# Pairing blocks of FFN channels: gate and value products over two PSUM banks, elementwise instructions over 1024 columns

## Chip, cores, metric

One core of one Trainium2 chip. Times are device microseconds (us) of that core, from the first to the last instruction of one execution. Times are medians of several executions; the profile is of one of them.

## The reference

```python
def mab(q, kv):                                  # attention, 4 batches of 12416 rows of 128
    s = (q @ kv.transpose(0, 2, 1)) / sqrt(C)
    a = softmax(s)
    return a @ kv
h = mab(I, x)                                    # 32 inducing rows attend to x
y = mab(x, h).reshape(B * N, C)                  # x attends to the 32 rows of h

xn = y / sqrt(mean(y * y) + 1e-6) * rms_g        # then a SwiGLU FFN over 49664 rows
g, val = xn @ w_gate, xn @ w_val                 # 128 -> 1536, twice
out = (silu(g) * val) @ w_out                    # 1536 -> 128
```

Almost all the work is the FFN: three products of 49664 x 128 x 1536, in fp32.

## The kernel before

Rows are handled in 100 units of up to 512 rows (25 a batch, 4 batches). The 1536 channels of a unit are 12 blocks of 128, so there are 1200 slots. In each slot TensorE does one gate product, one value product and, for a block that was finished some slots ago, one output product. ScalarE computes the SiLU, VectorE multiplies.

```python
ps_gv = pool("ps_gv", 4, space=PSUM)             # four tiles, of one bank each, in turn
...
for j in range(NJ):                              # 12 blocks of one unit
    g = ps_gv.tile([P, 512], F32, name="gv", tag="gv")
    nc.tensor.matmul(g[:, 0:T], sg[:, ts(j, P)], a[:, 0:T], start=True, stop=True)
    sl = silp.tile([P, 512], F32, name="silu")
    nc.scalar.activation(sl[:, 0:T], g[:, 0:T], AF.Silu)
    products(j)                                  # 0, 1 or 2 output products that are due
    v = ps_gv.tile([P, 512], F32, name="gv", tag="gv")
    nc.tensor.matmul(v[:, 0:T], sv[:, ts(j, P)], a[:, 0:T], start=True, stop=True)
    t = up.tile([P, 512], F32, name="u")
    nc.vector.tensor_tensor(out=t[:, 0:T], in0=sl[:, 0:T], in1=v[:, 0:T], op=ALU.mult)
    steps(j)                                     # attention of the next batch, seams, stores
```

PSUM is the memory into which TensorE puts its products; each of the four tiles above is one bank of it, 512 columns.

An output product is either plain (fp32) or split: the operand is converted into three parts of the type fp32r, and three matmuls of 0.23 us take the place of one of 0.85 us (the prediction reads both from the trace). The conversion takes two ScalarE copies and two GpSimd subtractions a block:

```python
def three(j, t):
    n = kws["n"] = (kws.get("n", 0) + 1) % 4
    hi, lo, d = (kws[name][:, n, 0:T] for name in ("hi", "lo", "d"))
    v = t[:, 0:T]
    nc.scalar.activation(hi, v, AF.Copy, scale=1.0 - 2.0 ** -13)
    nc.gpsimd.tensor_tensor(out=lo, in0=v, in1=hi.bitcast(F32), op=ALU.subtract)
    def rest():                                  # one slot later
        hs = third.tile([P, 512], F32, name="hs")
        nc.scalar.activation(hs[:, 0:T], hi.bitcast(F32), AF.Copy, scale=1.0 + 2.0 ** -12)
        nc.gpsimd.tensor_tensor(out=d, in0=hs[:, 0:T], in1=v, op=ALU.subtract)
        kara.append((ready[b, u, j], lambda: project3(j, hi, lo, d)))
```

A plan made ahead of time decides which blocks are converted: `SLOT` is the assumed length of a slot, `SPLIT` the GpSimd time of one conversion, `RESERVE` the number of due products above which a slot takes two. The plan converts 383 of the 1200 blocks and leaves 36 slots without an output product.

## Time and profile before

| | before |
|---|---|
| time, median | 1709.84 us (1709.16 to 1710.18, 3 runs) |
| first gate product | 59.8 us |
| loop, first to last gate product | 1640.7 us |
| of it TensorE's own work (matmuls at their pitches) | 1557.1 us |
| of it waits (the rest) | 83.6 us |
| after the last gate product | 7.6 us |

The loop's two parts are my arithmetic on the trace: the number of matmuls of each form times the start-to-start distance of that form where nothing waits, and what remains. The same prices are used for every kernel; what a lowered clock adds to matmuls counts as waits. TensorE's work is most of the time, so a kernel with the same work can win 84 us at most in the loop.

In the view of waits a line reads: engine, tile and line that waited, what ended the wait, then us in all, number of waits, and the longest.

### The profile page before, as it was taken

To read this page: it belongs to the slowest core of one execution; us is meant where nothing else is said; L and a number is where in the kernel's file an instruction comes from. 1 tells how busy PE (TensorE), PEld (TensorE's weight loads), DVE (VectorE), ACT (ScalarE), POOL (GpSimd) and SP (SyncE) were. 2 spreads that over 40 slices of the span, in tenths; PEclk is the share of its full clock that TensorE was granted. 3 is DMA by queue.
4 is the path that set the end of the run, shared out by engine and by line. 5 is a ranking of instruction groups with operands and counts; after the bars stand their busy time and mean duration, and the time that the engine had idled before them with its cause. 6 is when DMAs were issued, how large, how long until landed. Compare 5 with 4: busy or idle time off the path is not lost.

```text
span 1708.1 us, 23142 instructions
## 1 busy us (share of the span) xinstructions
PE 1668.0 (98%) x6781; PEld 1036.0 (61%) x6781; DVE 1145.0 (67%) x1914; ACT 1224.3 (72%) x2179; POOL 1146.2 (67%) x919
## 2 busy tenths in 40 slices
PE   8799999999999999999999999999999999999998
PEld 7445565655566666665556666566556666666666
DVE  4767775676667776667666777566756666666665
ACT  4446777676787777766678777767677887788786
POOL 1217775677587777677658777577657878887774
PEclk9899999999999999999999999999999999999999
DMA  6344533533354332433335314153211111111111
GB/s 261 74 68 75 70 80 60 121 75 69 56 78 68 49 65 51 105 75 88 65 57 90 57 34 87 28 131 79 54 31 33 35 36 33 33 36 36 33 37 24
DMA packets 389358, 112.64 MB, mean 66 GB/s; under 512 B 365136, under 2 KB 369776, under 8 KB 386672
## 3 DMA queue, kind: packets, MB, share of 16 engines
q1 hardware_dynamic: 388944, 111.02, 33.1%
q8 instruction: 54, 0.88, 0.2%
q14 instruction: 72, 0.59, 0.1%
q10 hardware_dynamic: 288, 0.15, 0.0%
HBM read 53.95 MB, written 27.00 MB: 47 GB/s over the span
## 4 chain that ended last, share of the span: by engine, by line
PE 87%; ACT 4%; DVE 3%; issue 2%; POOL 2%; DMA 1%; SPq 1%; ACTq 0%; DVEq 0%; POOLq 0%
PE acc L560 40%; PE gv L610 16%; PE gv L615 14%; PE u L578 5%; PE u L576 5%; PE mm L310 2%; DVE u L617 1%; PE mm L485 1%; ACT silu L612 1%; PE mm L368 1%; DVE aT L507 1%; PE gv L301 1%; ACT hi L510 1%; ACT hs L602 1%; POOL xn L603 1%
## 5 line engine op out<-in xcount | busy, mean ns | idle before, releaser
L617 DVE TENSOR_TENSOR u<-silu,gv 128x512 f32<-128x512 f32 (+2 forms) x1200 | 790.7, 666 | 512.1 <-PE gv L615 262.6
L612 ACT ACTIVATE silu<-gv 128x512 f32<-128x512 f32 (+2 forms) x1200 | 696.6, 584 | 370.1 <-PE gv L610 326.2
L560 PE MATMUL acc<-u,wo 128*128 128x512 f32 (+2 forms) x1634 | 811.5, 581 | 4.4 <-DVE u L617 3.1
L615 PE MATMUL gv<-a,sv 128*128 128x512 f32 (+2 forms) x1200 | 774.1, 645 | 3.7 <-DVE u L617 3.5
L598 POOL TENSOR_TENSOR xn<-u,xn 128x512 fp32r<-128x512 f32 (+2 forms) x383 | 482.2, 1259 | 356.0 <-ACT xn L597 295.1
L610 PE MATMUL gv<-a,sg 128*128 128x512 f32 (+2 forms) x1200 | 490.2, 409 | 12.8 <-ACT silu L612 8.5
L603 POOL TENSOR_TENSOR xn<-hs,u 128x512 fp32r<-128x512 f32 (+2 forms) x383 | 481.9, 1258 | 23.2 <-ACT hs L602 22.0
L610 PEld LDWEIGHTS gv<-a,sg 128*128 128x128 f32 x1200 | 227.2, 189 | 259.3 <-ACT silu L612 127.5
L560 PEld LDWEIGHTS acc<-u,wo 128*128 128x128 f32 x1634 | 305.1, 189 | 84.6 <-issue 18.2
L615 PEld LDWEIGHTS gv<-a,sv 128*128 128x128 f32 x1200 | 227.2, 189 | 204.1 <-issue 141.9
L597 ACT ACTIVATE xn<-u 128x512 fp32r<-128x512 f32 (+2 forms) x383 | 237.0, 619 | 15.6 <-DVE u L617 13.9
L602 ACT ACTIVATE hs<-xn 128x512 f32<-128x512 f32 (+2 forms) x383 | 235.7, 615 | 4.5 <-POOL xn L603 3.1
L560 PE MATMUL acc<-xn,xn 128*128 128x512 f32 (+2 forms) x383 | 149.7, 391 | 6.1 <-POOL xn L603 6.1
L578 PE MATMUL u<-xn,xn 128*128 128x512 f32 (+2 forms) x383 | 149.2, 390 | 0.0
L576 PE MATMUL u<-xn,xn 128*128 128x512 f32 (+2 forms) x383 | 147.8, 386 | 0.0
L499 POOL TENSOR_TENSOR rs<-ms,mhalf 128x16 f32<-128x16 f32 (+2 forms) x28 | 75.5, 2696 | 35.3 <-DVE ms L497 34.9
L560 PEld LDWEIGHTS acc<-xn,xn 128*128 128x128 f32 x383 | 71.8, 187 | 25.7 <-POOL xn L603 10.5
L578 PEld LDWEIGHTS u<-xn,xn 128*128 128x128 f32 x383 | 71.9, 188 | 15.6
L576 PEld LDWEIGHTS u<-xn,xn 128*128 128x128 f32 x383 | 72.1, 188 | 14.0
L569 DVE STREAM_TRANSPOSE o<-o 128x512 f32<-128x512 f32 (+2 forms) x97 | 67.7, 698 | 3.4
L568 DVE TENSOR_TENSOR o<-acc,o 128x512 f32<-128x512 f32 (+2 forms) x97 | 64.9, 669 | 0.0
L581 ACT ACTIVATE o<-u 128x512 f32<-128x512 f32 (+2 forms) x97 | 56.4, 581 | 0.2
(153 smaller groups left out, 735.0 us busy)
## 6 DMA issues: line engine op xcount, KB each, us to landing
out_dram<-o SPq DMA_DIRECT2D x320, 64.0 KB, 2.0
xT<-in_x_dram SPq DMA_DIRECT2D x60, 256.0 KB, 4.9
xn<-in_x_dram SPq DMA_DIRECT2D x60, 256.0 KB, 4.7
a<-hi SPq DMA_DIRECT2D x160, 64.0 KB, 2.0
a<-lo SPq DMA_DIRECT2D x158, 64.0 KB, 2.0
w<-w SPq DMA_DIRECT2D x22, 256.0 KB, 3.2
xn<-in_x_dram SPq DMA_DIRECT2D x5, 1024.0 KB, 10.9
out_dram<-o SPq DMA_DIRECT2D x64, 60.0 KB, 2.0
```

The source lines that it names most:

```text
L499: nc.gpsimd.tensor_tensor(out=rs, in0=ms, in1=mhalf[rows, 0:n], op=ALU.pow)
L560: nc.tensor.matmul(acc[:, 0:T], lhsT, rhs, start=st["left"] == NJ, stop=st["left"] == 1)
L576: nc.tensor.matmul(ups[:, 0:T], w[:, i, :], hi, start=st["k"] == nk, stop=False)
L578: nc.tensor.matmul(ups[:, 0:T], w[:, NK + i, :], lo, start=False, stop=not st["k"])
L597: nc.scalar.activation(hi, v, AF.Copy, scale=1.0 - 2.0 ** -13)
L598: nc.gpsimd.tensor_tensor(out=lo, in0=v, in1=hi.bitcast(F32), op=ALU.subtract)
L602: nc.scalar.activation(hs[:, 0:T], hi.bitcast(F32), AF.Copy, scale=1.0 + 2.0 ** -12)
L603: nc.gpsimd.tensor_tensor(out=d, in0=hs[:, 0:T], in1=v, op=ALU.subtract)
L610: nc.tensor.matmul(g[:, 0:T], sg[:, ts(j, P)], a[:, 0:T], start=True, stop=True)
L612: nc.scalar.activation(sl[:, 0:T], g[:, 0:T], AF.Silu)
L615: nc.tensor.matmul(v[:, 0:T], sv[:, ts(j, P)], a[:, 0:T], start=True, stop=True)
L617: nc.vector.tensor_tensor(out=t[:, 0:T], in0=sl[:, 0:T], in1=v[:, 0:T], op=ALU.mult)
```

## The change

The intent: ScalarE, VectorE and GpSimd pay a fixed part for every instruction (0.15 to 0.18 us, as the prediction works out from the trace), so handle two blocks with one instruction of 1024 columns. Gate products of a pair fill banks 0 and 1, value products banks 2 and 3. With the time saved on GpSimd the plan converts more blocks (470). Cut to its core:

```diff
-    SLOT, SPLIT, RESERVE = 1.25, 2.75, 3
+    SLOT, UPPER, SPLIT, RESERVE = 1.25, 2.6, 4.85, 3
-    ps_gv = pool("ps_gv", 4, space=PSUM)
+    ps_gv = pool("ps_gv", 1, space=PSUM)
+    gv = ps_gv.tile([P, 4, 512], F32, name="gv")
+    us = up.tile([P, 8, 512], F32, name="u")
     # one tile of the prologue:
-            return ps_gv.tile([P, 512], F32, name="gv", tag="gv")
+            kws["bank"] = (kws.get("bank", -1) + 1) % 4
+            return gv[:, kws["bank"], :]
     # the loop:
-        for j in range(NJ):
-            g = ps_gv.tile([P, 512], F32, name="gv", tag="gv")
-            nc.tensor.matmul(g[:, 0:T], sg[:, ts(j, P)], a[:, 0:T], start=True, stop=True)
-            ... SiLU, products(j), value product, multiplication, steps(j): one block
+        for j in range(0, NJ, 2):
+            pair = range(2)
+            for i in pair:
+                nc.tensor.matmul(gv[:, i, 0:T], sg[:, ts(j + i, P)], a[:, 0:T], start=True, stop=True)
+            sl = silp.tile([P, 2, 512], F32, name="silu")
+            nc.scalar.activation(sl[:, :, 0:T], gv[:, 0:2, 0:T], AF.Silu)
+            products(j)
+            for i in pair:
+                nc.tensor.matmul(gv[:, 2 + i, 0:T], sv[:, ts(j + i, P)], a[:, 0:T], start=True, stop=True)
+            slot = uslots.pop(0)
+            uslots.append(slot)
+            nc.vector.tensor_tensor(out=slot[0][:, :, 0:T], in0=sl[:, :, 0:T], in1=gv[:, 2:4, 0:T], op=ALU.mult)
+            steps(j)
+            products(j + 1)
+            steps(j + 1)
     # the conversion: hi, lo, hs and d over both blocks of a pair, rest() two slots later
     # cut: x rows of batches 1 to 3 loaded in halves into one buffer; z multiplied on VectorE
```

## The prediction

> **What bounds the kernel now.** I read the page's head first (busy shares), then its chain of waits, then ten microseconds of the timeline in the steady state, then the groups by form. The page first:
>
> ```profile
> PE 1668.0 (98%) x6781; PEld 1036.0 (61%) x6781; DVE 1145.0 (67%) x1914; ACT 1224.3 (72%) x2179; POOL 1146.2 (67%) x919
> PE 87%; ACT 4%; DVE 3%; issue 2%; POOL 2%; DMA 1%; SPq 1%; ACTq 0%; DVEq 0%; POOLq 0%
> ```
>
> TensorE is on 87% of the chain that ends last; no other engine has over 4%. The 98% is not proof, because matmul ends are modelled, so I take the period of a slot (one block of 128 FFN channels) from start to start in the timeline:
>
> ```profile
> 1003.20 0.39 PE L610 MATMUL gv<-a,sg 128*128 128x512 f32 x1
> 1003.43 1.02 PE L560 MATMUL acc<-u,wo 128*128 128x512 f32 x2
> 1003.88 0.79 PE L615 MATMUL gv<-a,sv 128*128 128x512 f32 x1
> 1004.51 0.40 PE L610 MATMUL gv<-a,sg 128*128 128x512 f32 x1
> 1004.75 0.39 PE L576 MATMUL u<-xn,xn 128*128 128x512 f32 x1
> 1004.98 0.40 PE L578 MATMUL u<-xn,xn 128*128 128x512 f32 x1
> 1005.21 0.39 PE L560 MATMUL acc<-xn,xn 128*128 128x512 f32 x1
> 1005.44 0.39 PE L615 MATMUL gv<-a,sv 128*128 128x512 f32 x1
> 1005.67 0.40 PE L610 MATMUL gv<-a,sg 128*128 128x512 f32 x1
> ```
>
> A slot whose output product is plain fp32 takes 1004.51 - 1003.20 = 1.31 us; one whose product is split into three fp32r matmuls takes 1005.67 - 1004.51 = 1.16 us, five matmuls 0.23 us apart. So a plain product costs 1.31 - 0.46 = 0.85 us, a split one 0.70 us, and a conversion gains 0.15 to 0.16 us. There is no gap in either slot: TensorE runs end to end.
>
> How much waiting is left? The loop runs from the first gate matmul at 59.8 us to the last at 1700.5: 1641 us. Its matmuls at those pitches (0.23 us for 512 columns, 0.217 for 480, 0.118 for 256): gate and value about 538; 817 plain products (642, 142 and 33 of the three widths) 546 + 114 + 14 = 674; 383 split ones (318, 50, 15) 221 + 33 + 5 = 259; the attention of the next batch, by the excess of the slots that hold it, about 88 (an estimate). Sum 1559, so some 82 us are waits, about 27 of them before 140 us, where the weights are still being prepared, and some 6 a batch around the two long exponentials.
>
> **What the Trainium skill says.** "TensorE: Matmul & The Clock Gate", section "Back-to-back issue gap", has N/2.4 + 2.5 ns, 216 ns at 512 columns. The plain product agrees if it is four passes (0.85/4 = 0.21 us); the fp32r matmuls here are at 0.23, and I use that. "VectorE: DVE Perf Modes", section on the TRN2 errata, has (N+151)/0.96 ns for an fp32 two-tensor operation: 691 at 512 (trace 682), 1224 at 1024. "ScalarE: Activation LUTs", "What ACT_TABLE_LOAD costs", has 186 + 0.833 N ns with immediate scale and bias: 613 at 512 (trace 597 to 631), 1039 at 1024. "GPSIMD Engine Reference", section 3.1, has about 2.6 cycles of 1.2 GHz an element for two inputs, 2.17 ns. The trace agrees, as the two widths of each group show:
>
> ```profile
> L617 DVE TENSOR_TENSOR u<-silu,gv 128x512 f32<-128x512 f32 x960 | 648.4, 682 | 409.0 <-PE gv L615 208.7 <-ACT hs L602 71.1 <-ACT xn L597 66.0
> L612 ACT ACTIVATE silu<-gv 128x512 f32<-128x512 f32 x960 | 570.6, 597 | 309.7 <-PE gv L610 269.2 <-DVE u L617 9.0 <-DVE xn L539 1.9
> L598 POOL TENSOR_TENSOR xn<-u,xn 128x512 fp32r<-128x512 f32 x318 | 410.2, 1290 | 272.5 <-ACT xn L597 219.8 <-PE gv L610 50.0 <-PE u L576 0.2
> L617 DVE TENSOR_TENSOR u<-silu,gv 128x256 f32<-128x256 f32 x48 | 19.4, 416 | 14.4 <-PE gv L610 5.5 <-PE gv L615 3.4 <-ACT silu L612 3.2
> L612 ACT ACTIVATE silu<-gv 128x256 f32<-128x256 f32 x48 | 18.2, 379 | 9.2 <-PE gv L610 9.0
> L598 POOL TENSOR_TENSOR xn<-u,xn 128x256 fp32r<-128x256 f32 x15 | 11.0, 733 | 10.2 <-ACT xn L597 10.1
> ```
>
> The number after each busy time is the mean of one instruction in ns. From 256 to 512 columns they grow by 266, 218 and 557 ns, so the fixed parts are only 150, 161 and 176 ns, and 1024 columns should take 1.21 us on VectorE, 1.03 on ScalarE and 2.40 on GpSimd.
>
> **The change, part by part.**
> *Elementwise work.* 1200 SiLU become 600: 1200 fixed parts of 0.16 become 600, ScalarE saves about 96 us; VectorE saves 600 x 0.15 = 90. Both are off the path, so this alone is worth next to nothing.
> *More split products.* The order in which the changed program's instructions compile has 470 split products (394, 64 and 12 of the three widths) where there were 383, and 730 plain ones for 817. TensorE saves 76 x 0.16 + 14 x 0.15 - 3 x 0.08 = 14.0 us. This is the one term that lies straight on the path. It is small: the pairing lets 87 more products convert, and each gives only a sixth of a slot. It isn't free: GpSimd does 235 pairs x 2 x about 2.35 = 1105 us for 964, ScalarE's two copies 490 for 473. GpSimd would then be busy about 1255 us (its multiplication of z, some 32 us, moves to VectorE), 74% of the span. It stays below TensorE.
> *Half the slack in PSUM.* Before, four single banks rotate, so a gate product waits for the SiLU of two slots earlier. Now gate and value have one pair of banks each. The next gate pair waits for this pair's SiLU: from the end of the second gate matmul 0.26 us until ScalarE starts (the timeline shows about that for an idle engine), 1.03 of work, 0.05 to pass on: 1.34 us. What TensorE has in between is the value pair (0.46) and the products placed around it. With two products that is 1.86 to 2.17 us: no wait. With none it waits 0.88 us. Likewise a value pair waits for the last multiplication, 0.26 + 1.21 + 0.05 = 1.52 us, against 0.46 plus the products. Counting in the compiled order the pairs without attention matmuls that fall short: 20 by a missing gate cover, 40 by a thin value cover of one product, together 29 us (some 9 us in each of the first three batches less the start, 2 in the last). The kernel before also has about 35 slots without a product, and pays about 0.4 us each, some 14 us, part of the 82.
> *Queues.* An operation of another kind in front of a multiplication now delays 1024 columns. In the compiled order about 30 stretches between two multiplications hold three VectorE instructions (2.1 us), some 25 hold four or five. With 1.21 for the multiplication, three make 3.3 against a pair's 2.3 to 2.6 plus a slack of 0.3 to 0.65: about 0.3 us lost each, 9 us; four or five lose 0.5 to 1.2 us (the squares' matmul there lengthens the pair), 17 us. The same clusters stand behind perhaps 25 of the 82 us now, in slots that run 0.2 to 0.5 us long.
> *The rest.* x rows of later batches are loaded in halves into one buffer five slots ahead, 6 us, for DMAs that land in 4.7 us now at twice the size, and their order lets them start earlier: no wait expected. The ramp before 59.8 us is unchanged; the last pair's drain is about 1 us longer.
> *Sum.* 1709.8 - 14 (split products) + 15 (thin pairs beyond what empty slots cost now) + 1 (clusters beyond now) + 1 (drain) = 1713. A reason to go lower: the schedule's constants look fitted to the new durations (4.85 us for two GpSimd instructions, which I get as 4.80), and the prologue and part of the thin pairs may be hidden by stalls that happen anyway, since two waits in the same place do not add. I take off half of the thin pairs' 15 us: 1705.
>
> **The rivals.**
> *A: overheads vanish and waiting shrinks.* With 186 us of fixed costs gone from ScalarE and VectorE, queues could be shorter, and the 55 us of waits after the ramp could fall by 20 to 30: 1665 to 1680. For it: waits on VectorE and ScalarE make up 7% of the chain. Against it: the longer single instruction and the halved bank rotation make each wait longer.
> *B: the rotation becomes the bound.* If SiLU or the multiplication regularly came late, each of 600 pairs would lose perhaps 0.1 to 0.2 us: 1750 to 1810. For it: only 0.3 us of slack where both products are split, and in the densest stretches ScalarE has 1.03 + 1.06 + 0.59 us a pair of about 2.4. Against it: the average pair is 2.6 us long.
> *C: GpSimd becomes the bound where conversions are dense.* 4.80 us for each two pairs of 4.9 to 5.2; a late difference blocks ScalarE's second copy, whose buffer is now single, and through it SiLU. The planner skips conversions when GpSimd is late, so I expect 5 to 10 us at the most from this: 1715.
>
> **Range and chances.** The sure term is -14, the unsure ones -10 to +25 in sum: 1688 to 1726 as 8 in 10, 1705 the middle. 2% faster would be under 1676, which needs rival A nearly in full; 2% slower, over 1744, needs rival B. Faster 0.05, within 2% 0.90, slower 0.05.
>
> **What would show it right or wrong.** Right: L652 near 1.21 us, L644 near 1.03, the two GpSimd lines near 2.40; a pair of gate starts about 2.62 us apart with two plain products, 2.31 with two split ones; new waits of TensorE's gate on SiLU and of its value pair on L652, of 20 to 50 us in all; TensorE still above 85% of the chain. Wrong: waits of gate or value matmuls above 60 us (rival B), split products waiting for GpSimd or ScalarE waiting for it by more than 15 us (rival C), or pair periods at the ideal nearly everywhere with waits well below today's (rival A). If instructions across two banks took longer than the slope says, the whole sum would be off upward.

## More of the kernel before

Before the change the gate product's weight load (PEld) waits for the SiLU that last read its bank, a short time:

```profile
PEld gv L610 <- ACT silu L612: 127.5, 458, 1.6
```

458 waits of 0.28 us on average. A weight load often waits while the matmul before it still runs, so most of this costs nothing: the gate matmuls themselves stood idle for that SiLU for 8.5 us in all.

## The result

The changed kernel takes 2565.16 us (2563.54 to 2567.95, 4 runs) against 1709.5 us for the kernel before in the same rounds: a ratio of 1.5007 (95% interval 1.4981 to 1.5033). Here and below the ratio is the mean time of one kernel's fast runs over that of the other's of the same rounds, so not quite the ratio of the medians quoted. The prediction said 1705. All outputs are right.

Busy times and the chain of waits of the changed kernel, in the order of the two lines that the prediction shows of before:

```profile
PE 2003.3 (78%) x6868; PEld 1019.7 (40%) x6868; DVE 1124.8 (44%) x1360; ACT 1181.8 (46%) x1282; POOL 1259.1 (49%) x596
PE 44%; DVE 26%; ACT 22%; issue 6%; DVEq 1%; POOL 0%; DMA 0%; ACTq 0%; POOLq 0%
```

No engine is busy for much more than three quarters of the span, and the chain that ends last is shared by three engines. That is the sign of work that goes round in a ring: not one engine is too slow, each waits for another. The groups say that the single instructions are as long as predicted (1.00 us for the SiLU and 1.19 for the multiplication, means over all widths; the 1024-column forms have 1.024 and 1.221):

```profile
L644 ACT ACTIVATE silu<-gv 128x1024 f32<-128x1024 f32 (+1 forms) x600 | 599.1, 999 | 1063.9 <-PE gv L642 1024.9
L652 DVE TENSOR_TENSOR u<-silu,gv 128x1024 f32<-128x1024 f32 (+2 forms) x482 | 574.5, 1192 | 1078.3 <-PE gv L647 1068.9
```

The waits name the ring:

```profile
PEld gv L647 <- ACT silu L644: 595.5, 592, 4.3
PEld gv L642 <- DVE u L652: 518.6, 461, 3.3
```

L642 is the gate pair, L644 its SiLU, L647 the value pair, L652 the multiplication. Both lines are wrong for a kernel with separate banks. The value product has no need of the SiLU: it writes other banks than the SiLU reads. The gate product of the next pair has no need of the multiplication. Yet 592 of 600 value pairs wait for the SiLU, and 461 gate pairs for the multiplication (115 more stand under another tile name of the product). In the timeline (start, length, engine, line; in brackets the idle time before and what ended it) one pair looks like this:

```profile
1504.08 0.74 PE L642 MATMUL gv<-a,sg 128*128 128x512 f32 x2 [0.52 <-DVE u L652]
...
1504.85 1.03 ACT L644 ACTIVATE silu<-gv 128x1024 f32<-128x1024 f32 x1 [2.00 <-PE gv L642]
...
1505.93 0.30 PEld L647 LDWEIGHTS gv<-a,sv 128*128 128x128 f32 x2 [0.16 <-ACT silu L644]
1506.04 0.62 PE L647 MATMUL gv<-a,sv 128*128 128x512 f32 x2
...
1506.80 1.22 DVE L652 TENSOR_TENSOR u<-silu,gv 128x1024 f32<-128x1024 f32 x1 [2.78 <-PE gv L647]
1508.08 0.30 PEld L642 LDWEIGHTS gv<-a,sg 128*128 128x128 f32 x2 [1.38 <-DVE u L652]
```

Gate pair at 1504.08, SiLU to 1505.88, value pair from 1505.93, multiplication 1506.80 to 1508.02, next gate pair at 1508.08: four steps in a row, 4.00 us, with no overlap among them. It does not matter what products TensorE does in between: 117 pairs with two plain products have a median period of 3.96 us, 90 pairs with two split ones 3.99. Predicted were 2.62 and 2.31. 600 pairs of 4 us make 2400 us.

| | before | changed | difference |
|---|---|---|---|
| first gate product | 59.8 | 101.7 | +42 |
| TensorE's own work in the loop | 1557.1 | 1541.6 | -15 |
| waits in the loop | 83.6 | 912.5 | +829 |
| after the last gate product | 7.6 | 8.9 | +1 |

The first line is, for the most part, the same cause in the prologue, whose transposes take their PSUM banks from the same tile (30 of the 42 us go with it in split_gv below). In the view by windows (columns: window, length, then busy us and number of instructions of PE, PEld, DVE, ACT and POOL, then the granted clock, DMA share and GB/s) the kernel before and the changed one have, from 10 to 60 us:

```profile
10.00:60.00 50.00, 45.52 (x497) 35.45 (x498) 31.70 (x70) 22.88 (x45) 8.02 (x5) 0.97 0.52 189
```

```profile
10.00:60.00 50.00, 32.15 (x123) 15.25 (x123) 8.75 (x22) 12.20 (x21) 2.54 (x2) 0.52 0.39 145
```

A quarter of the matmuls in the same time, and TensorE's clock granted at 0.52 instead of 0.97.

### The profile page after: what moved, and what is told of

Same layout as the page of the kernel before. It is cut to its first block, busy times and chain, and to the rows that moved or that the text cites. A ratio compares the mean times of both kernels' runs of the same rounds, so it can differ in the third digit from the quotient of the medians.

```text
span 2564.7 us, 21399 instructions
## 1 busy us (share of the span) xinstructions
PE 2003.3 (78%) x6868; PEld 1019.7 (40%) x6868; DVE 1124.8 (44%) x1360; ACT 1181.8 (46%) x1282; POOL 1259.1 (49%) x596
## 4 chain that ended last, share of the span: by engine, by line
PE 44%; DVE 26%; ACT 22%; issue 6%; DVEq 1%; POOL 0%; DMA 0%; ACTq 0%; POOLq 0%
ACT silu L644 20%; DVE u L652 17%; PE gv L647 16%; PE gv L642 15%; PE acc L579 6%; DVE xn L652 4%; PE mm L327 1%; PE u L595 1%; PE u L597 1%; PE mm L500 1%; PE gv L318 1%; DVE o L587 1%; DVE aT L523 1%; DVE o L588 1%; DVEq L652 1%
## 5 line engine op out<-in xcount | busy, mean ns | idle before, releaser
L644 ACT ACTIVATE silu<-gv 128x1024 f32<-128x1024 f32 (+1 forms) x600 | 599.1, 999 | 1063.9 <-PE gv L642 1024.9
L652 DVE TENSOR_TENSOR u<-silu,gv 128x1024 f32<-128x1024 f32 (+2 forms) x482 | 574.5, 1192 | 1078.3 <-PE gv L647 1068.9
L621 POOL TENSOR_TENSOR xn<-u,xn 128x1024 fp32r<-128x1024 f32 (+1 forms) x191 | 441.7, 2313 | 611.7 <-ACT xn L620 370.6
L642 PE MATMUL gv<-a,sg 128*128 128x512 f32 (+2 forms) x1200 | 455.2, 462 | 303.2 <-DVE u L652 237.8
L647 PE MATMUL gv<-a,sv 128*128 128x512 f32 (+2 forms) x1200 | 459.0, 465 | 222.7 <-ACT silu L644 222.7
L579 PE MATMUL acc<-u,wo 128*128 128x512 f32 (+2 forms) x1164 | 599.2, 600 | 1.0 <-POOL wo L279 1.0
L629 POOL TENSOR_TENSOR xn<-xn,u 128x1024 fp32r<-128x1024 f32 (+1 forms) x191 | 444.0, 2325 | 182.4 <-ACT xn L628 182.2
L642 PEld LDWEIGHTS gv<-a,sg 128*128 128x128 f32 x1200 | 190.6, 196 | 660.1 <-DVE u L652 518.6
L647 PEld LDWEIGHTS gv<-a,sv 128*128 128x128 f32 x1200 | 191.0, 195 | 605.8 <-ACT silu L644 595.5
L652 DVE TENSOR_TENSOR xn<-silu,gv 128x1024 f32<-128x1024 f32 (+2 forms) x118 | 138.7, 1176 | 258.5 <-PE gv L647 246.1
L628 ACT ACTIVATE xn<-xn 128x1024 f32<-128x1024 f32 (+2 forms) x235 | 242.6, 1032 | 0.0
L620 ACT ACTIVATE xn<-u 128x1024 fp32r<-128x1024 f32 (+1 forms) x191 | 197.1, 1032 | 62.3 <-PE u L595 62.3
L579 PE MATMUL acc<-xn,wo 128*128 128x512 f32 (+2 forms) x296 | 149.8, 589 | 0.4 <-DVE xn L652 0.4
```

The lines of the kernel that those rows point to most:

```text
L579: nc.tensor.matmul(acc[:, 0:T], lhsT, rhs, start=st["left"] == NJ, stop=st["left"] == 1)
L620: nc.scalar.activation(hi[:, :, 0:T], v, AF.Copy, scale=1.0 - 2.0 ** -13)
L621: nc.gpsimd.tensor_tensor(out=lo[:, :, 0:T], in0=v, in1=hi[:, :, 0:T].bitcast(F32), op=ALU.subtract)
L628: nc.scalar.activation(hs, hi[:, :, 0:T].bitcast(F32), AF.Copy, scale=1.0 + 2.0 ** -12)
L629: nc.gpsimd.tensor_tensor(out=d[:, :, 0:T], in0=hs, in1=v, op=ALU.subtract)
L642: nc.tensor.matmul(gv[:, i, 0:T], sg[:, ts(j + i, P)], a[:, 0:T], start=True, stop=True)
```

## The experiments

**Theory T** was that the four banks are one tile to the layer that records the program, and that it makes the waits for a tile as a whole: a write to bank 2 waits for the last reader of any bank of `gv`. The compiled program agrees: all 600 value pairs carry a wait for the SiLU of their own pair, and 595 of the 600 gate pairs one for the multiplication of the pair before. **The rivals**: the banks are waited for one by one and a pair of banks is simply too little (my prediction's rival B, R2 in the text below), an instruction that reads two banks keeps TensorE from writing the others (R1), or another part of the change costs the time (conversions, halved loads, z on VectorE). All the kernels below ran on chips next to the kernel before, whose median there was 1708.6 to 1709.5 us.

| run | median us | ratio to before (95%) |
|---|---|---|
| split_gv | 1798.57 | 1.0525 (1.0510 to 1.0541) |
| before_one_tile | 3452.64 (one run) | - |
| split_gv_alt | 1790.63 | 1.0477 (1.0461 to 1.0492) |
| unpaired_psum | 1749.35 | 1.0233 (1.0216 to 1.0250) |
| unpaired_r4 | 1745.07 | 1.0208 (1.0191 to 1.0225) |
| unpaired_s131_r3 | 1810.51 | 1.0590 (1.0571 to 1.0608) |
| unpaired_s131_r4 | 1801.75 | 1.0535 (1.0516 to 1.0555) |
| unpaired_halfcopies | 1752.08 | 1.0255 (1.0239 to 1.0271) |
| unpaired_halfall | 1740.38 | 1.0185 (1.0171 to 1.0199) |
| unpaired_sparse65 | 1733.25 | 1.0144 (1.0130 to 1.0157) |
| unpaired_stagger | 1747.85 | 1.0228 (1.0211 to 1.0245) |
| stagger_388 | 1722.71 | 1.0077 (1.0061 to 1.0093) |
| stagger_388_r3 | 1738.07 | 1.0171 (1.0156 to 1.0186) |
| stagger_dve | 1758.49 | 1.0289 (1.0275 to 1.0303) |
| unpaired_seam30 | 1738.42 | 1.0169 (1.0152 to 1.0186) |
| before_z | 1702.88 | 0.9967 (0.9955 to 0.9980) |
| before_zd | 1704.07 | 0.9973 (0.9959 to 0.9987) |

### split_gv: two tiles instead of one

```diff
-    gv = ps_gv.tile([P, 4, 512], F32, name="gv")
+    gvs = [ps_gv.tile([P, 2, 512], F32, name=n) for n in ("gvg", "gvv")]
-            return gv[:, kws["bank"], :]
+            return gvs[kws["bank"] // 2][:, kws["bank"] % 2, :]
     # gate, SiLU: gvs[0]; value, multiplication: gvs[1]
```

> The changed kernel, with its four PSUM banks as two tiles of two banks (gate, value) in place of one tile of four; same instructions, same order. Theory T: in the changed kernel the value pair waits for this pair's SiLU and the next gate pair for this pair's multiplication, because waits are made for a whole PSUM tile; banks that nobody else touches are waited for. Then this run falls to what my prediction added up, 1688 to 1726 us, the granted clock goes back to 0.99, and gate matmuls wait for SiLU alone and value matmuls for the multiplication alone, 20 to 50 us in all. Rival R1, an elementwise read across two PSUM banks keeps TensorE from writing the others: stays near 2560. Rival R2, one pair of banks each is too little to rotate with, whatever the tiles: over 1750.

Measured: 1798.57 us. Nothing but the tile that the banks belong to was changed (TensorE's instructions stand in the same order in both traces), and 767 of the 856 us are gone. The waits now have the right names, the value pair waiting for the multiplication and the gate pair for the SiLU:

```profile
PEld gvv L647 <- DVE u L652: 116.1, 268, 3.4
PEld gvg L642 <- ACT silu L644: 69.0, 71, 4.3
```

In the compiled program no value pair waits for a SiLU any more, and 599 of the 600 gate pairs wait for the SiLU of the pair before. First gate product at 72.1 us, waits in the loop 171.7 us. So T is shown, for the most part of the loss (741 us of it in the loop, 30 in the prologue, by the profiled executions), and R1, which stays near 2560, fell. But T's figure of 1688 to 1726 us was missed, and the time is over R2's mark of 1750. What is left is 89 us.

### before_one_tile: the same fault in the kernel before

```diff
-    ps_gv = pool("ps_gv", 4, space=PSUM)
+    ps_gv = pool("ps_gv", 1, space=PSUM)
+    gv4 = ps_gv.tile([P, 4, 512], F32, name="gv")
-            g = ps_gv.tile([P, 512], F32, name="gv", tag="gv")     # and v, and the prologue's
+            g = gv_bank()                                          # gv4[:, turn % 4, :]
```

> The kernel before, with its four single-bank PSUM tiles for gate and value as one tile of four banks used in the same rotation; no pairs, no wide instructions. T: a slot becomes a chain, gate 0.23 + 0.26 to start ScalarE + SiLU 0.60 + 0.05, value 0.23 + 0.26 + multiplication 0.68 + 0.05, 2.36 us a slot; times 1164 slots of 512 columns, and 68 us around the loop, about 2810 us. R1 and R2 need the 1024-column instructions or fewer banks: 1710 us.

Measured: 3452.64 us, one run. No pairs here, no longer conversions: the tile alone doubles the time of the kernel before. (A pair does the ring once for two blocks, so the single blocks suffer more.) The waits:

```profile
PEld gv L617 <- DVE u L624: 1453.2, 1191, 2.8
PEld gv L622 <- ACT silu L619: 664.2, 1106, 4.2
PE gv L617 <- DVE u L624: 862.2, 1105, 2.4
```

Of 1200 gate products 1191 wait for the multiplication, as T says. The size was not what I had worked out, 2810 us. The granted clock accounts for about half of that. In the slices of the span, in tenths of full speed:

```profile
PEclk6878988997589997998758998999776898998855
```

The mean was 0.828 (0.995 in the kernel before). I had put in matmuls at full speed. A slot of 512 columns with one plain product takes 2.47 us where the trace has the clock at full speed (median of 439), near my 2.36, and 3.71 us where it is halved (34 such slots). By such a comparison of all slots the lowered clock costs some 300 of the 640 us that I was short (an estimate from these slots); the rest is slots longer than 2.36 us at full clock, and the prologue (first gate product at 102.1 us).

### split_gv_alt and unpaired_psum: the halved rotation

split_gv_alt is split_gv with the prologue's banks taken from the two tiles in turn:

```diff
-            return gvs[kws["bank"] // 2][:, kws["bank"] % 2, :]
+            return gvs[kws["bank"] % 2][:, kws["bank"] // 2, :]
```

> split_gv, but the ramp before the loop takes its PSUM banks alternately from the two tiles, where split_gv takes both banks of one tile in a row. If waits are made for a whole PSUM tile also between the banks of a two-bank tile, split_gv's ramp is serialised by halves (its first gate matmul starts at 72.1 us, 58.1 in unpaired_psum), and this run starts its loop near 60 us and takes 1785 to 1790 us. If the ramp's delay has another cause: 1798 again.

Measured: 1790.63 us, 8 less; the first gate product is at 65.3 us instead of 72.1. unpaired_psum gives gate and value back their four single banks in turn, one block an instruction for SiLU and multiplication; conversions stay in pairs of 1024 columns:

```diff
+            for i in pair:
+                g = ps_gv.tile([P, 512], F32, name="gv", tag="gv")
+                ... gate product, SiLU into sl[:, i, 0:T]
+                products(j + i)
+                v = ps_gv.tile([P, 512], F32, name="gv", tag="gv")
+                ... value product, multiplication into slot[0][:, i, 0:T]
+                steps(j + i)
```

> The changed kernel's conversions in pairs (470 split products, 1024-column copies and differences on SBUF), but gate, value, SiLU and multiplication one block at a time over four rotating single-bank tiles, as before. Nothing waits for a bank it does not use, and the rotation is as deep as before. T with my sum: -14 us of TensorE work against the kernel before and no loss by thin pairs, 1690 to 1705 us; it should be 5 to 20 us below split_gv, which is what the halved rotation costs. If the conversions in pairs bring waits of their own (GpSimd 2.4 us an instruction), 1705 to 1730 us. R1: also near 1700, so this run does not speak on it.

Measured: 1749.35 us, 41 below split_gv_alt, though it does 600 more instructions on each of two engines. It was to be 1690 to 1705, or 1705 to 1730 with waits for the conversions: both missed. First gate product 58.1 us against 65.3, waits 139.5 us against 171.1. So even with proper waits the pairing costs 41 us: 7 in the prologue, which has four single banks in turn again, 31 in the loop and 2 after it in the profiled executions. That TensorE has less to do, with two banks a side, while it waits for the longer instruction is the likely reason in the loop. It is not shown apart: this run shortens the instructions, deepens the rotation and puts the output products at other places, all at once.

What is left is 40 us over the kernel before, with 14 us less of TensorE work: 56 us more of waits. This is the residual, and all the rest is about it. Its first candidate: the paired plan leaves 98 slots without an output product, 36 before.

### unpaired_r4, unpaired_s131_r3, unpaired_s131_r4: slots without a product

```diff
-    SLOT, UPPER, SPLIT, RESERVE = 1.25, 2.6, 4.85, 3      # unpaired_psum: 470 conversions, 98 empty slots
+    SLOT, UPPER, SPLIT, RESERVE = 1.25, 2.6, 4.85, 4      # unpaired_r4: 470, 65
+    SLOT, UPPER, SPLIT, RESERVE = 1.31, 2.6, 4.85, 3      # unpaired_s131_r3: 482, 226
+    SLOT, UPPER, SPLIT, RESERVE = 1.31, 2.6, 4.85, 4      # unpaired_s131_r4: 482, 73
```

> unpaired_psum with the stock of products that is kept back raised from 3 to 4. The same 470 split products, but in the compiled order 65 slots without an output product in place of 98 (the kernel before has 36). Theory E: a slot without a product costs 0.57 us (62 such slots of the loop lose 35.6 us in unpaired_psum), since gate and value alone don't cover the way through SiLU and the multiplication: 33 x 0.57 = 19 us less, about 1730 us. Rival: the 40 us over the kernel before are waits for GpSimd's long instructions or for the halved row loads, and stay: 1745 to 1752.

> unpaired_psum planned with slots of 1.31 us: 482 split products in place of 470 (2 us less of TensorE work), but 226 slots without a product, each next to one with two. Theory E: 128 more such slots at 0.4 to 0.57 us, 50 to 73 us more, about 1800 to 1820 us. Rival (uneven products cost nothing): 1747.

> The same 482 split products as unpaired_s131_r3, stock kept back 4: 73 slots without a product. Theory E: close to unpaired_r4, 1730 to 1740 us, 70 to 85 us below unpaired_s131_r3 with equal work on every engine. Rival: equal to it.

Measured: 1745.07, 1810.51 and 1801.75 us. unpaired_s131_r3 landed where theory E put it, but by luck: the theory, that each empty slot costs about half a microsecond, fell with the other two. 33 empty slots fewer are worth 4 us (the runs of unpaired_r4 spread over 7), 153 fewer 9 us. The waits moved to slots that do have a product. But the denser plan of 482 conversions, with 73 empty slots, is 52 us slower than unpaired_psum with 98 (its plan also assumes longer slots). So look at the conversions.

### unpaired_halfcopies, unpaired_halfall: is it the length of one instruction?

```diff
-            nc.scalar.activation(hi[:, :, 0:T], v, AF.Copy, scale=1.0 - 2.0 ** -13)
+            for i in range(2):
+                nc.scalar.activation(hi[:, i, 0:T], v[:, i, :], AF.Copy, scale=1.0 - 2.0 ** -13)
     # hs likewise; in unpaired_halfall also lo and d on GpSimd
```

> Unpaired gate and value (1749.35 us, 1.0233 of the kernel before), but each of the two ScalarE conversion copies of a pair is written as two instructions of 512 columns (about 0.6 us each) instead of one of 1024 (1.05 us). GpSimd keeps its 1024 columns. Theory G1, a SiLU stands behind a long copy in ScalarE's queue and the gate product two slots on waits for it: the 62 us of TensorE waits that go to the SiLU fall to about 40 and the time to about 1730 (1.012). Theory G2, what is late is the GpSimd result and not the SiLU: within 5 us of 1749. Theory R, the rest of the loss is the halved row loads and the plan's order, not the length of an instruction: within 5 us of 1749 too. TensorE's own work is the same, 1543 us in the loop, in all.

> The same, and the two GpSimd instructions of a pair are two of 512 columns each as well (about 1.27 us instead of 2.37). The first half of a pair's low part and difference is ready 1.1 us earlier. G1: as the last, 1730, for GpSimd adds under 3 us. G2: the waits that go to GpSimd, 11.5 us of the loop, and some of those under the products fall, so that this is 10 us or more below the last. R: within 5 us of 1749.

Measured: 1752.08 and 1740.38 us. Halving ScalarE's copies in place does nothing (G1's figure was 1730). Halving GpSimd's wins 9 us over unpaired_psum and 12 over unpaired_halfcopies, as G2 said.

### unpaired_sparse65: fewer conversions

```diff
-    SLOT, UPPER, SPLIT, RESERVE = 1.25, 2.6, 4.85, 3      # 470 conversions, 98 empty slots
+    SLOT, UPPER, SPLIT, RESERVE = 1.25, 2.6, 6.5, 3       # 268 conversions, 56 empty slots
```

> Unpaired gate and value with the spacing between two conversions in the plan raised from 4.85 to 6.5 us: 268 split products instead of 470. TensorE's own work grows by about 202 x 0.22 = 44 us, to about 1587 us in the loop. G (both): the waits beyond it, 139.5 us now, fall in step with the 202 conversions fewer, by about 55 us x 202/470 x 2 or so = 45 us, so the time stays near 1749 (1735 to 1760). R: the waits stay near 139 us, so the time is about 1793 (1.049).

Measured: 1733.25 us. TensorE has 33 us more to do (1575.6 us; I had put 44), and the kernel is 16 us faster all the same: waits 88.5 us instead of 139.5. Rival R, at 1793, fell. In these plans conversions beyond some number cost more in waits than the 0.16 us that each saves TensorE; the empty slots fell too, from 98 to 56.

### unpaired_stagger and stagger_388: bunching or number?

The halved copies of the last pair of runs still stand side by side ahead of the same SiLU, so that test of bunching was poor. unpaired_stagger puts them one slot apart, with TensorE's order the same instruction by instruction:

```diff
+            head(0)                                # hi, lo of the first block
+            soon(1, lambda: head(1))               # of the second, one slot later
+            soon(2, lambda: rest(0))               # hs, d
+            soon(3, lambda: rest(1))
-    SLOT, UPPER, SPLIT, RESERVE = 1.25, 2.6, 4.85, 3      # unpaired_stagger: 470 conversions, 98 empty slots
+    SLOT, UPPER, SPLIT, RESERVE = 1.25, 2.6, 5.4, 4       # stagger_388: 388, 67
```

> Unpaired gate and value, the same 470 conversions, TensorE's order unchanged instruction for instruction; but each conversion instruction covers one block of 512 columns and the two blocks of a pair are one slot apart, so that one copy (0.6 us) stands between two SiLUs where two (1.2 us, or one of 1.05) stood. Theory B, bunching: it is the elementwise work of two blocks standing together in ScalarE's order that makes a SiLU late; the 61 us of waits that go to the SiLU fall to 30 to 40 and the time from 1740 (all halved in place) to 1712 to 1722. Theory D, density: it is the 470 conversions as such; within 5 us of 1740.

> The same with the spacing of two conversions raised to 5.4 us and the reserve to 4: 388 split products, nearly the 383 of the kernel before, and 67 slots without a product (36 before). TensorE's own work is then 1556 us in the loop against 1557 before. B and D: waits of 85 to 100 us, as before has 84, so 1708 to 1724 us (1.0 to 1.009). Theory R, the halved row loads or another part of the change that all these kernels share: the waits stay near 125 to 130 us and the time near 1747.

Measured: 1747.85 and 1722.71 us. B, bunching, fell: one copy between two SiLUs is no better than two together (1740.38 in unpaired_halfall; D's figure, within 5 us of that, was missed by 3). R's figure for stagger_388, 1747, fell as well. With about the number of conversions of the kernel before the residual is down from 40 to 13 us: waits 97.0 us, TensorE's own work 1556.0. Since both the number and the empty slots changed, one more run was needed.

### stagger_388_r3: number or empty slots?

```diff
-    SLOT, UPPER, SPLIT, RESERVE = 1.25, 2.6, 5.4, 4       # stagger_388: 388 conversions, 67 empty slots
+    SLOT, UPPER, SPLIT, RESERVE = 1.25, 2.6, 5.4, 3       # 388 conversions, 125 empty slots
```

> stagger_388 (1722.71 us, 67 slots without a product, reserve 4) with the reserve back at 3: the same 388 conversions, but 125 slots without a product. If the number of conversions is what counts: within 6 us of 1723. If it is the empty slots (58 more, up to 0.5 us each): 1738 to 1750, as unpaired_stagger with its 470 conversions and 98 empty slots had 1748.

Measured: 1738.07 us. Of the 25 us between unpaired_stagger and stagger_388, 10 come with the smaller number (at 27 more empty slots), 15 with 58 fewer empty slots, 0.26 us a slot. So both count. Together with unpaired_r4 (33 slots, 4 us) it means that an empty slot has no fixed price: it costs where something else is late there.

### stagger_dve: is GpSimd full?

In the last quarter of the run, where no attention of a next batch is in the way, GpSimd is the busiest engine after TensorE. The last line of the view by windows, eight windows of 30 us from 1420 to 1660, for the kernel before, unpaired_psum, unpaired_stagger and stagger_388:

```profile
sum 240.00, PE 239.55 PEld 154.78 DVE 153.66 ACT 192.46 POOL 190.40; mean PE 29.94 PEld 19.35 DVE 19.21 ACT 24.06 POOL 23.80
```

```profile
sum 240.00, PE 235.15 PEld 153.02 DVE 158.76 ACT 188.12 POOL 218.34; mean PE 29.39 PEld 19.13 DVE 19.85 ACT 23.52 POOL 27.29
```

```profile
sum 240.00, PE 232.04 PEld 152.91 DVE 153.81 ACT 199.33 POOL 227.78; mean PE 29.00 PEld 19.11 DVE 19.23 ACT 24.92 POOL 28.47
```

```profile
sum 240.00, PE 240.00 PEld 155.48 DVE 158.57 ACT 189.07 POOL 196.03; mean PE 30.00 PEld 19.43 DVE 19.82 ACT 23.63 POOL 24.50
```

POOL is at 79, 91, 95 and 82% of 240 us; TensorE has gaps just where POOL is above 90%. In unpaired_stagger ScalarE even waits for GpSimd to give its buffer back, with the next SiLU behind it:

```profile
ACT xn L628 <- POOL xn L629: 20.6, 13, 2.3
```

That is a correlation, so I took load off GpSimd:

```diff
-                nc.gpsimd.tensor_tensor(out=d[:, i, 0:T], in0=hs[:, i, :], in1=v[:, i, :], op=ALU.subtract)
+                (nc.vector if i and n else nc.gpsimd).tensor_tensor(out=d[:, i, 0:T], ...)
```

> unpaired_stagger (1747.85 us, 470 conversions, waits of 135.5 us beyond TensorE's own 1542.7) with every fourth difference d moved from GpSimd (1.27 us) to VectorE (about 0.67 us): GpSimd loses 117 x 1.27 = 149 us, VectorE (67% busy) gains 78 us, ScalarE and TensorE's order are unchanged. Theory P, GpSimd is full where conversions are dense: its share in the last quarter falls from 95% to about 85% and the waits to 95 to 110, so 1708 to 1723 us. Theory S, ScalarE is what has no room (two copies a conversion ahead of the SiLU): within 6 us of 1748. VectorE getting in the way instead: above 1754.

Measured: 1758.49 us, 11 slower, waits 148.0 us. In the same windows:

```profile
sum 240.00, PE 232.97 PEld 153.75 DVE 169.22 ACT 199.29 POOL 204.17; mean PE 29.12 PEld 19.22 DVE 21.15 ACT 24.91 POOL 25.52
```

GpSimd's share fell to 85%, as meant, and TensorE did not gain. This is the outcome that the text above gives as "VectorE getting in the way": in the view of waits TensorE's own (PE) waits for SiLU and multiplication rise from 36 to 46 us in all, while those for GpSimd's difference fall from 18 to 14. That a moved subtraction stands ahead of a multiplication is the likely reason, but it was not tested apart. So a full GpSimd is not shown to be the cause; what is shown is that taking a tenth of its load away this way doesn't help.

### unpaired_seam30: a meeting of two delays

In the last quarter of unpaired_psum the waits over 0.9 us are nearly all in one place that comes back every fourth unit: block 11, a slot without a product, at the last step of a seam (the steps that make the next tile of rows ready for the FFN), where that tile's activations are transposed (aT) and copied (hi):

```profile
1464.11 0.80 PE L650 MATMUL gv<-a,sv 128*128 128x512 f32 x1
1464.55 0.69 DVE L521 STREAM_TRANSPOSE aT<-sc 128x512 f32<-128x512 f32 x1
1464.75 0.39 PE L646 MATMUL gv<-a,sg 128*128 128x512 f32 x1
1464.97 0.40 PE L650 MATMUL gv<-a,sv 128*128 128x512 f32 x1
1465.27 0.62 ACT L524 CAST hi<-aT 128x512 fp32r<-128x512 f32 x1 [2.03 <-DVE aT L521]
...
1465.80 0.59 ACT L647 ACTIVATE silu<-gv 128x512 f32<-128x512 f32 x1
...
1466.44 0.50 PE L646 MATMUL gv<-a,sg 128*128 128x512 f32 x1 [1.07 <-ACT silu L647]
```

ScalarE stood idle for 2.03 us at a copy whose input VectorE had not transposed yet, with the SiLU behind it in the same queue. TensorE had only 0.46 us of work in this slot and waits 1.07 us; the next gate product starts 1.69 us after this one, so in a slot with a product (1.16 or 1.31 us) it would have waited some 0.4 to 0.5 us (an estimate from these times).

```diff
-                j = ((14, 17, 18, 21, 21, 33) if k else (32, 33, 33, 34, 34, 37))[i]
+                j = ((14, 17, 18, 21, 21, 30) if k else (32, 33, 33, 34, 34, 37))[i]
```

> unpaired_psum (1749.35 us) with the last step of each seam, the transpose and split of the next tile's activations, three slots earlier (30 instead of 33), so that in the last quarter it no longer meets the empty slot at block 11; 83 slots without a product in all instead of 98, 470 conversions as before. Theory C, meetings of an empty slot with a seam step: some 25 seams at 0.6 to 1 us, so 1725 to 1735 us, and the last quarter's waits fall from 16.3 us to about 11. Else: within 5 us of 1749.

Measured: 1738.42 us, 11 below unpaired_psum. In the last quarter the waits in block 11 fall from 6.6 to 1.1 us, and 2.5 of the 5.5 come back in blocks 8 and 9, where the seam now is: 13.7 us there in all, from 16.3. The mechanism is shown at this place, where both kernels have the same empty slots; its size is about half of what C said. The 11 us of the whole run are not its price alone: the new plan also has 83 empty slots in place of 98, all 15 of them before the last quarter.

### before_z and before_zd: one part alone, in the kernel before

```diff
-            nc.vector.transpose(out=z[rows, :, :].rearrange("p t m -> p (t m)"), in_=ps[rows, 0:w])
-            engine.tensor_tensor(out=z[rows, :, :], in0=z[rows, :, :], in1=weights(b, s), op=ALU.mult)
+            flat = z[rows, :, :].rearrange("p t m -> p (t m)")
+            nc.vector.tensor_tensor(out=flat, in0=ps[rows, 0:w], in1=st["eT"][rows, 0:w], op=ALU.mult)
+            nc.vector.transpose(out=flat, in_=flat)
-                seam_busy[at] = seam_busy.get(at, 0) + {2: 1.4, 3: 3.0, 4: 1.2, 5: 1.4}.get(i, 0)
+                seam_busy[at] = seam_busy.get(at, 0) + {3: 3.0, 4: 1.2, 5: 1.4}.get(i, 0)
     # before_zd: also SPLIT 2.75 -> 2.2, and every fourth difference d on VectorE
```

> The kernel before with one part of the change alone: the z multiplication moved from GpSimd to VectorE (product read from PSUM, then a transpose in place) and its reservation of GpSimd's time taken out, so that the plan takes 403 split products instead of 383, all of them single blocks. TensorE's own work falls by 20 x 0.22 = 4.4 us. If nothing else gives way: 1704 to 1706 us (0.997). If VectorE's longer seam delays its multiplications: 1710 to 1716. Either way this part is not what cost the change its 856 us.

> before_z (1702.88 us, 403 single conversions) with every fourth difference d on VectorE and the spacing of two conversions cut from 2.75 to 2.2 us, so that the plan takes 426. TensorE's own work falls by 23 x 0.163 = 3.8 us, GpSimd's load falls by 106 x 1.26 - 23 x 2.52 = 76 us. P: 1697 to 1700 us. S: the additional copies on ScalarE cost as much as they win, 1702 to 1710.

Measured: 1702.88 us (1701.87 to 1705.92, 5 runs), 0.9967 of the kernel before, and 1704.07 us, 0.9973. before_z takes a part of the change that is good by itself: GpSimd has 403 conversions instead of 383, TensorE 3.2 us less to do, and the waits are 80.0 us instead of 83.6. It beats the kernel before by a third of a per cent. before_zd's 426 conversions save TensorE 3.7 us more and lose it again: waits 84.7 us. P's figure, 1697 to 1700, was missed. So with single blocks the plan seems to be near its best number of conversions already; before_zd also moves differences to VectorE, and the two were not tested apart.

## Why the prediction was wrong

The step that failed is **"Half the slack in PSUM"**, in its sentence "The next gate pair waits for this pair's SiLU". It took the four banks as four things to wait for. In the compiled program it is the other way round: the gate pair waits for the multiplication and the value pair for this pair's SiLU. I had the lists of waits at hand when I predicted, each instruction with the engine it waits for. I looked at whether the regions of PSUM were apart and did not ask of one value product which instruction it waits for. I priced that step at 29 us, 15 of them new; the false waits were worth 767.

Point by point:

- **Durations: right.** 1221 ns for the multiplication (1.21 predicted), 1024 for the SiLU (1.03), 2367 and 2379 for GpSimd (2.40).
- **TensorE's own work: right.** -14 predicted, -15 found.
- **Rotation, even without the fault: mis-sized.** split_gv, which has the waits that I assumed, is at 1798.57 us. Pairing gate and value costs 41 us (split_gv_alt against unpaired_psum), 33 of them in the loop and after it, where I had put +15 and halved it. So without the fault the prediction would have been wrong too. The time lies in rival B's band of 1750 to 1810, but that is partly luck: of the 89 us over the kernel before, only these 33 can be what B described.
- **"The ramp before 59.8 us is unchanged": wrong.** +42 us in the changed kernel, +12 in split_gv, +5.5 in split_gv_alt, none in unpaired_psum. I had not asked which PSUM tile the prologue's transposes use.
- **More split products, "each gives only a sixth of a slot", a gain: wrong in sign.** They do save 0.16 us each (that is an eighth of a slot of 1.31 us, not a sixth). But with 470 planned in pairs and 98 empty slots there are 56 us more of waits than before (unpaired_psum); with 388 and 67, 13 more (stagger_388). Rival C named the engines; my 5 to 10 us for it were too little.
- **"I take off half of the thin pairs' 15 us": not supported.** There was nothing that hid them.
- **The range:** its own terms, -14 and then -10 to +25, make 1686 to 1721 us, not 1688 to 1726.

The loss adds up by runs: 767 us for the tile that all banks share (to split_gv), 8 for the prologue's order of banks (to split_gv_alt), 41 for gate and value in pairs, 7 of them in the prologue (to unpaired_psum), 40 for the conversion plan and what comes with it. Of the last, 27 go with stagger_388 (fewer conversions about 10, fewer empty slots about 15, the rest is within the scatter). **What stays open**: the last 13 us, and why more conversions make TensorE wait. Length of the instruction, bunching ahead of a SiLU and GpSimd's load have each been tested and none explains it alone; the one mechanism that I could point to in a trace, an empty slot that meets a seam step, is worth 11 us at most (unpaired_seam30, with 15 empty slots fewer). The halved row loads were never tested by themselves; stagger_388 has them too, so they can hardly cost more than the last 13 us there, unless another part makes up for it.

On the hardware side nothing asked for the false waits. The Trainium skill, "PSUM — Partial Sum Buffer", section "PSUM bank collisions raise a hardware error", says that two engines on different banks run clean and gives the rule to guard PSUM by bank and quadrant. The runs agree: split_gv drops the waits across banks, is correct, and is 767 us faster.

## What to carry to other kernels

Separate banks give overlap only if they are separate tiles for whatever makes the waits: before merging small tiles into one large one, take one instruction of each kind in the compiled program and name what it waits for. When no engine is busy all the time and the chain of waits is shared by three, look for a ring, and check its period against the work inside it. And a saving on a side engine is worth only what the main engine then does sooner: here longer instructions, fewer buffers and more conversions together took back more than they gave.

## What the Trainium skill lacked or had wrong

- "PSUM — Partial Sum Buffer": it says what the hardware requires (guard by bank and quadrant), not that the program's waits may be coarser. One tile over four banks cost 767 of 2565 us here, and doubled the kernel before (3453 us against 1709). No page of the skill has it.
- "TensorE: Matmul & The Clock Gate", section "Why this matters for your kernels": it asks for no idle gaps over about 3 us. In before_one_tile, after the first 107 us, no matmul stood idle for more than 2.4 us before it started, and yet the trace has the clock halved 85 times, for 1106 us (mean over the run 0.828; in the changed kernel 0.947, and 0.52 in its prologue). The same page's section "A second HAM failure mode: psum-queue depth-cycling" does say that short idle times between groups of matmuls make the clock change; no page gives a share of busy time at which it does. Which gaps did it is not settled here.
- "TensorE: Matmul & The Clock Gate", section "Back-to-back issue gap": it gives about 216 ns for an isolated matmul of 512 columns and about 131 ns for a stream of matmuls with weight loads, and does not name fp32r. The fp32r matmuls of a split product, each with its own weight load, start 0.23 us apart here at full granted clock (1004.75, 1004.98, 1005.21 in the timeline that the prediction shows).
